# A mixer block with an FFT convolution: step two's matrix loaded twice from 64 rows, and a new order of loads and work in the first chunk

## The chip, the cores and the metric

The kernel runs on one core of a Trainium2 chip. Such a core has five engines with queues of their own: TensorE (matrix products; loading weights and streaming the moving operand are separate instructions), VectorE, ScalarE, GpSimd (called POOL in the profile) and SyncE, which here only issues transfers. SBUF is the working memory of 128 partitions, PSUM holds TensorE's results. The metric is device time in microseconds (us) of one execution, lower is better.

## The reference

Inputs are q, k, v of 2048 tokens × 640 channels, all float32. The reference, cut to what matters:

```python
def _A_ref(q, k, v, shift_k, ssm_k, ssm_D):
    k_shift = sum(k_pad[:, t:t + S, :] * shift_k[:, ks - 1 - t] for t in range(ks))   # ks = 4
    kv = k_shift * v
    kv_f = rfft2(kv_pad); kf_f = rfft2(kf_pad)           # length 2 S = 4096, per channel
    y = irfft2(kv_f * kf_f)[:S] + kv * ssm_D
    return q * y

x = A_q
sa, ca, ga, sb, cb, gb = split(_silu(c) @ w_mod, 6)      # "modulation", 640 each
h = _layernorm(x) * (1 + ca) + sa
x = x + ga * _A_ref(h, A_k, A_v, A_shift_k, A_ssm_k, A_ssm_D)
h = _layernorm(x) * (1 + cb) + sb
x = x + gb * _B_ref(h, B_w1, B_b1, B_w2, B_b2)           # MLP over tokens, hidden size 1728
```

## The kernel before

**Tiling.** The 640 channels are worked in five chunks of 128 (`NC`, `DC`), one after the other. Each chunk's K·V product and its filter go through a Fourier transform that is written as two matrix steps, are multiplied, and come back through two inverse steps. After the fifth chunk follow the second layer norm and the MLP, which the change does not touch.

**One chunk.** The stages, with the lines that the profile gives:

- `kv_ops(g)` (L59, four groups g): the short convolution times v, eight operations a group, into `X` (tile x). Groups 0, 1 and 3 run on VectorE with the taps copy `TAP` in PSUM, group 2 on POOL with the taps copy `PW` in SBUF. `taps()` and `all_taps()` make these copies, and `load_taps`, `load_k`, `load_v`, `load_halo` load what they read. `kv_loads(c, g)` issues the loads for the next chunk behind group g.
- `step1(side, t)` (L218): step one, side 0 from `X`, side 1 (the filter) from `KSP` (tile p); 32 matmuls for each of four t, whose moving operand is the constant `F1`. The weights of side 0 are a view of `X` whose 64 columns lie 32 floats apart; those of side 1 lie side by side. ScalarE copies each result to `T_z` (L220).
- `load_ks`, `perm_add`, `perm` bring the filter of a chunk: load, add `ssm_D` to one row, and reorder on ScalarE (L164).
- `f2(g)` (L234): step two, eight groups of 64 matmuls. The weights are 64 columns of the constant matrix `T_w2` (two tiles of 128 × 4096, the tiles w0 and w1 of the trace's w), the moving operand is a view of `T_z`. Each weight slice is loaded twice in a row, once for each half of the output partitions. Then ScalarE copies a part out (L238), VectorE multiplies (p), and POOL adds (y), VectorE in the last group of chunks one to four.
- `i2` (L263) and `i1` (L282): the inverse steps. `i1` uses the constant `V1`, whose place `T_v1` also holds pieces of `w_mod` in the first chunk.
- `gate` multiplies by the normalised x (`A1`, made by the operations `ac` on ScalarE and `po` on VectorE) and adds into x on POOL; `spill` writes x away.

**The first chunk** also computes the layer norm's statistics (L536, L537), `rstd`, and the first half of the modulation: `mod_load` (w_mod, five parts), `mod_part` (products, L342), `mod_sum`, `mod_row` (L353 to L369). In it, `step1(0, t)` for the second chunk runs right behind the first chunk's step two, and `step1(1, t)` for the second chunk at its end.

**Order.** The schedule is written by hand: every engine's queue holds its instructions in the order of the program, and each waits for what it reads or overwrites. `fill` is a list of VectorE operations (the next chunk's `kv_ops`), and `dv(n)` puts the next n of them into the program. SyncE's queue holds nearly all transfers, so a transfer that waits holds up those behind it; a few early ones are issued from ScalarE's queue. PSUM results rotate through three slots (`psum()`), and `tap` is a fourth of its own that holds the taps and also the modulation's sum.

**The matrix.** The constant `c_w2` has 128 rows of 8192 floats. A row stands for a part (real or imaginary), an index n2 and a channel parity; half of its entries are zero, because a channel's outputs take nothing from the other parity.

Of the kernel before, what the change touches and what calls it, by code (L numbers as in the profile page):

```python
# [11 lines left out]
AF = mybir.ActivationFunctionType  # L12
# [8 lines left out]
def _constants():  # L21


    n1, n2, k1, k2 = np.arange(64), np.arange(32), np.arange(64), np.arange(32)
    a = 2 * np.pi * ((1 + 4 * k1)[None, :] * n1[:, None] % 256) / 256
    f1 = np.zeros((2, 64, 2, 2, 64))
    for h in range(2):
        f1[h, :, 0, h], f1[h, :, 1, h] = np.cos(a), np.sin(a)
    ang = 2 * np.pi * ((1 + 4 * k1)[None, :, None] * n2[:, None, None] / 8192
                       + (k2[None, None, :] * n2[:, None, None] % 32) / 32)  # L30
    w2 = np.zeros((2, 32, 2, 64, 2, 2, 32))
    for c in range(2):
        w2[0, :, c, :, 0, c] = np.cos(ang)
        w2[1, :, c, :, 0, c] = -np.sin(ang)
        w2[0, :, c, :, 1, c] = np.sin(ang)
        w2[1, :, c, :, 1, c] = np.cos(ang)
    ang = 2 * np.pi * (k2[:, None] * n2[None, :] % 32) / 32
    c, s = np.cos(ang), np.sin(ang)
    v2 = np.tile(np.concatenate([c, -s, s, c], 1), (4, 1))
    ang = 2 * np.pi * ((1 + 4 * k1)[:, None, None] * (32 * n1[None, None, :] + n2[None, :, None]) % 8192) / 8192  # L40
    v1 = np.tile(np.stack([np.cos(ang), np.sin(ang)], 1).reshape(64, 4096) / 2048, (2, 1))
    sel = np.zeros((128, 128))
    sel[0, 0:64] = sel[1, 64:128] = 1
    small = np.concatenate([f1.reshape(128, 256), v2, np.eye(128)[:, 0:36], sel], 1)
    return {"small": small.astype(np.float32), "w2": w2.reshape(128, 8192).astype(np.float32),
            "v1": v1.astype(np.float32)}


# [1 line left out]
def mixer_kernel(ctx: ExitStack, tc: tile.TileContext, q, k, v, shift_k, ssm_k, ssm_D, w1, b1, w2, b2, c,  # L50
# [24 lines left out]
    def dram(t, offset, ap):  # L75
        return bass.AP(tensor=t.tensor, offset=t.offset + offset, ap=ap)
# [18 lines left out]
    Z = T_z.rearrange("p (s t a k e) -> p s t a k e", s=2, t=4, a=8, e=2)  # L95
    T2 = T_z[:, 4096:8192].rearrange("p (a m e) -> p a m e", a=32, e=2)
    Y = T_y.rearrange("p (r i k) -> p r i k", r=2, i=32)
    W2 = [t.rearrange("p (k m) -> p k m", m=64) for t in T_w2]
    V1 = T_v1[:, 0:4096].rearrange("p (r n m) -> p r n m", r=2, n=32)
    SM = T_v1[:, 4096:4516]  # L100
    F1, V2, ID = SM[:, 0:256], SM[:, 256:384], SM[:, 384:420]
# [44 lines left out]
    def load_taps(c, eng=sync):  # L146
        for h in range(2):
            eng.dma_start(TR[64 * h:64 * h + 64], dram(shift_k, (DC * c + 64 * h) * 4, [[0, 64], [1, 256]]))
# [75 lines left out]
    def f2(g):  # L224

        ps = psum()
        for kk in range(8):
            k1 = 8 * g + kk
            for ri in range(2):
                for h in range(2):  # L230
                    o = 128 * kk + 64 * ri
                    rhs = bass.AP(tensor=T_z.tensor, offset=T_z.offset + 128 * h + 2 * k1,
                                  ap=[T_z.ap[0], [256, 32], [1, 2]])
                    pe.matmul(ps[64 * h:64 * h + 64, o:o + 64], W2[k1 // 32][:, 2 * (k1 % 32) + ri], rhs, start=True, stop=True)  # L234
        pv = ps.rearrange("p (m s i) -> p m s i", s=2, i=32)
        xs_ = pv[:, :, 0]
        kt = KT[g % 2]
        act.activation(kt.rearrange("p (m i) -> p m i", i=32), pv[:, :, 1], AF.Copy)  # L238
        pa, pb = P[:, 1024 * (g % 2):1024 * (g % 2) + 512], P[:, 1024 * (g % 2) + 512:1024 * (g % 2) + 1024]
        m16 = lambda t: t.rearrange("p (m i) -> p m i", i=32)  # L240

        def mul():
            TT(dve, m16(pa), xs_, m16(kt), ALU.mult)
            sw = bass.AP(tensor=kt.tensor, offset=kt.offset + 32, ap=[kt.ap[0], [64, 8], [-32, 2], [1, 32]])
            TT(dve, pb.rearrange("p (k r i) -> p k r i", k=8, r=2), xs_.rearrange("p (k r) i -> p k r i", r=2), sw,
               ALU.mult)
# [187 lines left out]


    piece = lambda t, n: [t[:, 640 * i:640 * i + 640] for i in range(n)]
    stg = T_g[0:36, 0:128]
    dve.memset(stg, 0.0)
    dve.memset(ones, 1.0)
    dve.memset(msk, 1.0)  # L440
    dve.memset(msk[0:32], 0.0)
    dve.memset(epsc, EPS)
    for h in range(2):
        dve.memset(KX[64 * h:64 * h + 1, 0:3, :], 0.0)
    both = (sync, act)
# [13 lines left out]
    def run(ops):  # L459
        for f_ in ops:  # L460
            f_()
# [2 lines left out]
    all_taps()  # L464
    load_taps(1, act)
    run(kv_ops(2, pool))
    run(kv_ops(0))
    kv_loads(1, 0)
    run(kv_ops(1))
    kv_loads(1, 1)  # L470
    kv_loads(1, 2)
    run(kv_ops(3))
    sync.dma_start(T_w2[0], c_w2[:, 0:4096], max_dma_last_dim=4096)
    kv_loads(1, 3)
    sync.dma_start(T_w2[1], c_w2[:, 4096:8192], max_dma_last_dim=4096)
    for h in range(2):
        sync.dma_start(stg[7 * h:7 * h + 6, :], dram(b1, 864 * h, [[128, 6], [1, 128]]))
        sync.dma_start(stg[7 * h + 6:7 * h + 7, :], dram(b1, 864 * h + 736, [[128, 1], [1, 128]]))
    sync.dma_start(stg[14:30, :], dram(b2, 0, [[128, 16], [1, 128]]))
    sync.dma_start(stg[30:35, :], dram(c, 0, [[128, 5], [1, 128]]))  # L480
    perm_add(0)
    perm(0)
    all_taps()
    load_taps(2)
    for t in range(4):
        step1(0, t)
    run(kv_ops(2, pool))
# [2 lines left out]
    for t in range(4):  # L490
        step1(1, t)

    for j in range(0, 16, 2):
        for b in range(2):
            sync.dma_start(XH[j // 8][64 * b:64 * b + 64, j % 8:j % 8 + 2],
                           dram(q, (16 * b + j) * D, [[32 * D, 64], [D, 2], [1, D]]))
# [14 lines left out]
    for c in range(NC):  # L511
# [30 lines left out]
        if c == 0:  # L542
            mod_load(0, 4, P[:, 0:1920])
            for t in range(4):
                step1(0, t)
            ps = psum()
            pe.transpose(ps[:, 0:36], stg, ID[0:36, 0:36])
            act.activation(cols, ps[:, 0:36], AF.Copy)
            act.activation(sil, cols[:, 30:35], AF.Silu)
            i2(0)  # L550
            for kk in range(4):
                mod_part(tap, kk, pl[kk])
                if kk == 0:
                    load_ks(1)
            sync.dma_start(T_v1[:, 0:4096], c_v1, max_dma_last_dim=4096)
            rstd(rs1, nm1, 0, 16)
            run(ac[0:4])
            i2(1)
            mod_part(tap, 4, pl[4])
            load_k(2, 1)  # L560
            load_k(2, 2)
            load_v(2, 2)
            load_halo(2)
            load_k(2, 0)
            load_v(2, 0)
            load_v(2, 1)
            load_k(2, 3)
            load_v(2, 3)
            mod_sum(tap, T_kt[:, 0:640])
            run(ac[4:8])  # L570
            pool.tensor_scalar(PW, TR.rearrange("p (i s) -> p s i", s=4), 1.0, None, op0=ALU.mult)
            run(kv_ops(2, pool))
            for i in range(3):
                mod_row(i, T_kt[:, 0:640])
            taps()
            load_taps(3)
            perm_add(1, dve)
            perm(1)
            load_ks(2)
            run(ac[8:16])  # L580
            run(po[0:2])
            fill.extend(kv(3, ((0,), (1, 2), (3,))))
        elif cn is not None:
            for t in range(2):
                step1(0, t)
            perm(cn)
            if c + 2 < NC:
                fill.extend(kv(c + 3 if c + 3 < NC else None))
            else:
                fill.extend(x1s(cc, j) for cc in range(c) for j in range(16))  # L590
        else:
            blk.update({f: (j16(t[:, 0:2048]), j16(t[:, 2048:4096])) for f, t in (
                (0, mem("w0", 4096, "wb0")), (1, mem("w1", 4096, "wb1")))})
            mod_load(3, 3, T_z[:, 0:1920])
            mod_load(3, 4, P[:, 0:1920])
            for kk in range(3):
                mod_part(tap, kk, pl[kk])
            t = mem("in", 4288, "wb3")
            blk[3] = j16(t[:, 0:2048]), j16(t[:, 2048:4096])
            split_rows(0, X, (0, 1, 3))  # L600
            split_rows(1, T_aux[:, 0:2048], (0, 1, 3))
            run(po)
# [36 lines left out]
        spill(c)  # L639
        if c:  # L640
            k0()
        for t in range(1 if c else 0, 4):
            step1(1, t)
        if cn == NC - 1:
# [24 lines left out]
    start = []  # L669
# [410 lines left out]
```

## Time and profile before

| what | us |
|---|---|
| median of 3 runs (lowest, highest) | 722.62 (722.25, 728.29) |
| the profiled execution's own time | 726.87 |
| its span, first to last instruction | 725.0 |
| step two of the second chunk begins | 115.58 |
| step two of the third, fourth, fifth chunk begins | 166.47, 216.14, 273.93 |
| mean granted TensorE clock | 0.968 |

In a group line of the profile stand the source line, the engine, the operation, the tile written and the tiles read, the shapes and the count; then the busy time with the mean length of one in ns; then the idle time of the engine just ahead, and what ended it. `PE` is TensorE's matmul, `PEld` its weight load, `SPq` and `ACTq` are issues in SyncE's and ScalarE's queue. A timeline row has start and length in us, and merges neighbours of one kind (x32: 32 of them); in square brackets stands the idle time before it. Since matmuls overlap in time, the length of one says little about their rate.

### The profile page before, as it was taken

Reading aid. Unit: us, or ns where it says so; the run is one execution under the profiler, and the core shown is the slowest. Engines: PE = TensorE matmul, PEld = TensorE weight load, DVE = VectorE, ACT = ScalarE, POOL = GpSimd, SP = SyncE. Lnnn points to the kernel's source line nnn. Section 1 sums busy time; section 2 is a strip of 40 time slices with the busy share of each in tenths; the row PEclk is TensorE's granted clock in tenths of the full one; section 3 lists DMA queues with packets and bytes.
Section 4 is the critical chain, followed back from the end, with each engine's and each line's share of the span. In section 5 each row is a group of like instructions: output and inputs, shape, how many; then the busy total and the mean of one; then the engine's idle time right before and its main releaser. Section 6 shows DMA issues by size and latency. Waiting matters only on the chain.

```text
span 725.0 us, 20744 instructions
## 1 busy us (share of the span) xinstructions
PE 655.3 (90%) x9131; PEld 633.1 (87%) x9131; DVE 493.4 (68%) x861; ACT 297.1 (41%) x461; POOL 155.0 (21%) x135
## 2 busy tenths in 40 slices
PE   0797969999999989888799999999999989999997
PEld 0797759989989979767799999999999989999997
DVE  7766658969878537878895312311399868878887
ACT  0532565645645535544766313212335222332222
POOL 5197048625428226300000000000000000000000
PEclk9999889999999889989999999999999999999999
DMA  9989998345423440352112453353163433455410
GB/s 187 242 232 233 298 230 178 91 75 140 87 65 114 113 107 15 111 114 63 29 31 59 80 95 60 59 105 70 51 189 103 129 100 117 140 157 175 149 54 37
DMA packets 165807, 84.89 MB, mean 117 GB/s; under 512 B 88883, under 2 KB 157270, under 8 KB 165718
## 3 DMA queue, kind: packets, MB, share of 16 engines
q1 hardware_dynamic: 161170, 82.27, 45.8%
q10 hardware_dynamic: 4548, 1.31, 1.1%
q8 instruction: 71, 1.16, 0.7%
q14 instruction: 18, 0.15, 0.1%
HBM read 73.07 MB, written 10.49 MB: 115 GB/s over the span
## 4 chain that ended last, share of the span: by engine, by line
PE 53%; DVE 24%; issue 6%; ACT 6%; POOL 4%; DMA 4%; SPq 2%; ACTq 0%; DVEq 0%; POOLq 0%
PE pst L432 21%; PE pst L218 9%; PE pst L1021 7%; PE pst L234 6%; PE pst L263 5%; DVE m_w L59 4%; POOL y L59 4%; PE pst L282 3%; DVE m_x L59 3%; DVE tap L59 2%; ACT m_w L934 2%; PE pst L946 2%; DVE kt L59 2%; DVE m_v L59 1%; DVE m_x L955 1%
## 5 line engine op out<-in xcount | busy, mean ns | idle before, releaser
L234 PE MATMUL pst<-z,w 128*64 128x64 f32 x2560 | 96.2, 240 | 10.6 <-ACT z L220 6.1
L234 PEld LDWEIGHTS pst<-z,w 128*64 128x64 f32 x2560 | 94.8, 141 | 12.4 <-ACT z L220 7.3
L59 POOL TENSOR_TENSOR y<-p 128x256 f32<-128x256 f32 x72 | 91.2, 1319 | 28.3 <-DVE p L59 27.9
L59 DVE TENSOR_TENSOR p<-pst,kt 128x512 f32<-128x512 f32 x80 | 52.7, 691 | 29.6 <-ACT kt L238 20.3
L218 PE MATMUL pst<-v,x 128*64 128x128 f32 x640 | 48.0, 312 | 23.6 <-DVE x L59 23.2
L220 ACT ACTIVATE z<-pst 128x1024 f32<-128x1024 f32 x40 | 45.8, 1145 | 55.3 <-PE pst L218 33.7
L218 PEld LDWEIGHTS pst<-v,x 128*64 128x64 f32 x640 | 45.7, 221 | 24.3 <-POOL t L457 23.2
L238 ACT ACTIVATE kt<-pst 128x512 f32<-128x512 f32 x40 | 25.2, 629 | 57.6 <-PE pst L234 37.7
L825 ACT ACTIVATE pst<-pst,sm 128x640 f32<-128x640 f32 x14 | 10.7, 767 | 85.9 <-PE pst L432 85.9
L263 PEld LDWEIGHTS pst<-v,y 32*128 32x128 f32 x1280 | 40.8, 198 | 5.9 <-POOL y L59 2.7
L263 PE MATMUL pst<-v,y 32*128 32x64 f32 x1280 | 42.9, 284 | 2.7 <-DVE y L59 1.9
L946 PE MATMUL pst<-r_z,m_w 128*128 128x320 f32 x222 | 42.8, 312 | 2.2 <-DVE m_w L59 1.7
L218 PE MATMUL pst<-v,p 128*64 128x128 f32 x640 | 40.0, 284 | 2.2 <-issue 2.2
L218 PEld LDWEIGHTS pst<-v,p 128*64 128x64 f32 x640 | 37.5, 143 | 3.4 <-issue 2.9
L934 ACT ACTIVATE m_w<-m_v 128x896 fp32r<-128x896 f32 x24 | 22.2, 949 | 42.3 <-DVE m_v L59 29.4
L946 PEld LDWEIGHTS pst<-r_z,m_w 128*128 128x128 f32 x222 | 34.9, 189 | 3.8 <-DVE m_w L59 3.0
L59 DVE TENSOR_TENSOR tap<-tap,kt 128x512 f32<-128x512 f32 x51 | 35.6, 698 | 1.3
L59 DVE TENSOR_TENSOR kt<-in,tap 128x512 f32<-128x512 f32 x51 | 35.0, 686 | 1.4
L282 PEld LDWEIGHTS pst<-z,v 64*64 64x64 f32 x1280 | 23.6, 152 | 11.7 <-issue 6.2
L282 PE MATMUL pst<-z,v 64*64 64x64 f32 x1280 | 25.3, 238 | 9.3 <-issue 4.9
L59 DVE TENSOR_TENSOR m_w<-m_v,m_w 128x896 fp32r<-128x896 f32 x24 | 26.0, 1087 | 10.4 <-ACT m_w L934 10.4
L271 ACT ACTIVATE z<-pst 128x512 f32<-128x512 f32 x38 | 21.2, 657 | 26.4 <-PE pst L263 26.4
(276 smaller groups left out, 1422.5 us busy)
## 6 DMA issues: line engine op xcount, KB each, us to landing
x<-in_B_w_dram SPq DMA_DIRECT2D x24, 512.0 KB
m_v<-in_B_w_dram SPq DMA_DIRECT2D x15, 384.0 KB
x<-in_B_w_dram SPq DMA_DIRECT2D x14, 384.0 KB
aux<-in_A_ssm_k_dram SPq DMA_DIRECT2D x10, 512.0 KB
in<-in_A_k_dram SPq DMA_DIRECT2D x36, 128.0 KB
in<-in_A_v_dram SPq DMA_DIRECT2D x36, 128.0 KB
m_x<-xs SPq DMA_DIRECT2D x28, 160.0 KB
out_dram<-m_x SPq DMA_DIRECT2D x28, 160.0 KB
```

What stands on the lines that cost most here:

```text
L59: TT = lambda eng, o, a, b, op: eng.tensor_tensor(o, a, b, op=op)
L218: pe.matmul(ps[64 * ri:64 * ri + 64, o:o + 128], lhs, F1[:, 128 * ri:128 * ri + 128], start=True, stop=True)
L220: evac = lambda: act.activation(Z[:, side, t].rearrange("p a k e -> p e a k"), ps.rearrange("p (e a k) -> p e a k", a=8, e=2), AF.Copy)
L234: pe.matmul(ps[64 * h:64 * h + 64, o:o + 64], W2[k1 // 32][:, 2 * (k1 % 32) + ri], rhs, start=True, stop=True)
L238: act.activation(kt.rearrange("p (m i) -> p m i", i=32), pv[:, :, 1], AF.Copy)
L263: pe.matmul(pp[qd // 2][:, o:o + 64], Y[p, ri, i:i + 2].rearrange("p i k -> p (i k)"), V2[p, 64 * ri:64 * ri + 64], start=ri == 0, stop=ri ...
L271: act.activation(o, i, AF.Copy)
L282: pe.matmul(ps[64 * b:64 * b + 64, 512 * e + 64 * jj:512 * e + 64 * jj + 64], V1[p, ri, n2], T2[p, :, 32 * ri + n2], start=ri == 0, stop=r ...
L432: pe.matmul(ps[0:m, h, 0:320], w_.bitcast(F32R), r_[:, 320 * h:320 * h + 320].bitcast(F32R), start=first and i == 0, stop=last and i == 2)
L934: act.activation(W[n][0].bitcast(F32R), a(w_), AF.Copy)
L946: pe.matmul(bank[n], w[:, i].bitcast(F32R), r.bitcast(F32R), start=i == 0 and k == 0, stop=i == 6 and k == 2)
L1021: pe.matmul(acc[s][:, h, 0:320], w[:, f_].bitcast(F32R), u[r + h].bitcast(F32R), start=f_ == 0 and k == 0, stop=f_ == NF - 1 and k == 2)
```

## The change

Six things are done. The zeros of the matrix are no longer loaded: the constant has 64 rows of 4096, each half of it is written twice, into the even and the odd partitions of a tile that POOL has set to zero. So that both copies are runs of memory, the tile's columns now lie with the matrix's column as the outer index: a weight slice's 64 columns lie 64 floats apart (`w2_of`). The order of transfers in the first chunk is new: the first half of the matrix ahead of the second chunk's K and V, the second half behind all of them, the biases, c and a set of taps moved from there into the loop over q, and q loaded one row index at a time (32 transfers in place of 16). 72 matmuls whose result nobody reads stand ahead of the first step one, and a small ScalarE copy stands at the start. Inside the first chunk, the third chunk's K and V, its POOL group and 16 VectorE operations are moved ahead, the second filter's load behind that of `V1`, and its `perm_add`, `perm` and the next filter's load behind the gate work. The modulation's sum uses a rotating PSUM slot instead of `tap`.

```diff
-    w2 = np.zeros((2, 32, 2, 64, 2, 2, 32))
...
+    w2 = np.zeros((2, 32, 64, 2, 32))
+    w2[0, :, :, 0], w2[1, :, :, 0] = np.cos(ang), -np.sin(ang)
+    w2[0, :, :, 1], w2[1, :, :, 1] = np.sin(ang), np.cos(ang)
...
-    W2 = [t.rearrange("p (k m) -> p k m", m=64) for t in T_w2]
+    def w2_of(k1, ri):
+        return T_w2[k1 // 32].rearrange("p (m k) -> p k m", m=64)[:, 2 * (k1 % 32) + ri]
+
+    def load_w2c(i):
+        for e in range(2):
+            sync.dma_start(T_w2[i][e::2, 2048 * e:2048 * e + 2048], c_w2[:, 2048 * i:2048 * i + 2048],
+                           max_dma_last_dim=4096)
...
-                    pe.matmul(ps[64 * h:64 * h + 64, o:o + 64], W2[k1 // 32][:, 2 * (k1 % 32) + ri], rhs, start=True, stop=True)
+                    pe.matmul(ps[64 * h:64 * h + 64, o:o + 64], w2_of(k1, ri), rhs, start=True, stop=True)
...
+    pool.memset(T_w2[0], 0.0)
     stg = T_g[0:36, 0:128]
...
     dve.memset(epsc, EPS)
+    act.activation(tm[:, 0:1], epsc, AF.Copy)
...
     run(kv_ops(2, pool))
+    pool.memset(T_w2[1], 0.0)
+    load_w2c(0)
     run(kv_ops(0))
...
     run(kv_ops(3))
-    sync.dma_start(T_w2[0], c_w2[:, 0:4096], max_dma_last_dim=4096)
     kv_loads(1, 3)
-    sync.dma_start(T_w2[1], c_w2[:, 4096:8192], max_dma_last_dim=4096)
-    (b1, b2 and c into stg: six transfers)
+    load_w2c(1)
     perm_add(0)
     perm(0)
     all_taps()
-    load_taps(2)
+    ps = psum()
+    for i in range(72):
+        pe.matmul(ps[0:64, 0:128], F1[:, 0:64], F1[:, 128:256], start=True, stop=True)
...
-    for j in range(0, 16, 2):
+    for j in range(16):
         for b in range(2):
-            sync.dma_start(XH[j // 8][64 * b:64 * b + 64, j % 8:j % 8 + 2],
-                           dram(q, (16 * b + j) * D, [[32 * D, 64], [D, 2], [1, D]]))
+            sync.dma_start(XH[j // 8][64 * b:64 * b + 64, j % 8], dram(q, (16 * b + j) * D, [[32 * D, 64], [1, D]]))
+        if j == 11:
+            (b1, b2 and c into stg: six transfers)
+            load_taps(2)
...
+            taps()
+            pool.tensor_scalar(PW, TR.rearrange("p (i s) -> p s i", s=4), 1.0, None, op0=ALU.mult)
             i2(0)
-            for kk in range(4):
-                mod_part(tap, kk, pl[kk])
-                if kk == 0:
-                    load_ks(1)
-            sync.dma_start(T_v1[:, 0:4096], c_v1, max_dma_last_dim=4096)
-            rstd(rs1, nm1, 0, 16)
-            run(ac[0:4])
-            i2(1)
-            mod_part(tap, 4, pl[4])
             load_k(2, 1)
...
             load_v(2, 3)
-            mod_sum(tap, T_kt[:, 0:640])
+            load_taps(3)
+            mt = psum()
+            for kk in range(4):
+                mod_part(mt, kk, pl[kk])
+            sync.dma_start(T_v1[:, 0:4096], c_v1, max_dma_last_dim=4096)
+            load_ks(1)
+            rstd(rs1, nm1, 0, 16)
+            run(kv_ops(2, pool))
+            run(ac[0:4])
+            i2(1)
+            mod_part(mt, 4, pl[4])
+            mod_sum(mt, T_kt[:, 0:640])
+            fill.extend(kv(3, ((0,), (1, 2), (3,))))
+            dv(16)
             run(ac[4:8])
-            pool.tensor_scalar(PW, TR.rearrange("p (i s) -> p s i", s=4), 1.0, None, op0=ALU.mult)
-            run(kv_ops(2, pool))
             for i in range(3):
                 mod_row(i, T_kt[:, 0:640])
-            taps()
-            load_taps(3)
-            perm_add(1, dve)
-            perm(1)
-            load_ks(2)
             run(ac[8:16])
             run(po[0:2])
-            fill.extend(kv(3, ((0,), (1, 2), (3,))))
...
         if c:
             k0()
+        else:
+            perm_add(1, dve)
+            perm(1)
+            load_ks(2)
```

More of the change, by code (lines that the diff above doesn't have):

```diff
@@ L30, in _constants @@
                        + (k2[None, None, :] * n2[:, None, None] % 32) / 32)
-    w2 = np.zeros((2, 32, 2, 64, 2, 2, 32))
[L32 to L36, printed above, removed]
+    w2 = np.zeros((2, 32, 64, 2, 32))
+    w2[0, :, :, 0], w2[1, :, :, 0] = np.cos(ang), -np.sin(ang)
+    w2[0, :, :, 1], w2[1, :, :, 1] = np.sin(ang), np.cos(ang)
     ang = 2 * np.pi * (k2[:, None] * n2[None, :] % 32) / 32
@@ L44, in _constants @@
     small = np.concatenate([f1.reshape(128, 256), v2, np.eye(128)[:, 0:36], sel], 1)
-    return {"small": small.astype(np.float32), "w2": w2.reshape(128, 8192).astype(np.float32),
+    return {"small": small.astype(np.float32), "w2": w2.reshape(64, 2, 64, 32).transpose(0, 1, 3, 2).reshape(64, 4096).astype(np.float32),
             "v1": v1.astype(np.float32)}
@@ L472, in mixer_kernel @@
     run(kv_ops(3))
-    sync.dma_start(T_w2[0], c_w2[:, 0:4096], max_dma_last_dim=4096)
     kv_loads(1, 3)
-    sync.dma_start(T_w2[1], c_w2[:, 4096:8192], max_dma_last_dim=4096)
[L476 to L480, printed above, removed]
+    load_w2c(1)
     perm_add(0)
@@ L491, in mixer_kernel @@
         step1(1, t)
-    for j in range(0, 16, 2):
+    for j in range(16):
         for b in range(2):
-            sync.dma_start(XH[j // 8][64 * b:64 * b + 64, j % 8:j % 8 + 2],
-                           dram(q, (16 * b + j) * D, [[32 * D, 64], [D, 2], [1, D]]))
+            sync.dma_start(XH[j // 8][64 * b:64 * b + 64, j % 8], dram(q, (16 * b + j) * D, [[32 * D, 64], [1, D]]))
+        if j == 11:
+            for h in range(2):
+                sync.dma_start(stg[7 * h:7 * h + 6, :], dram(b1, 864 * h, [[128, 6], [1, 128]]))
+                sync.dma_start(stg[7 * h + 6:7 * h + 7, :], dram(b1, 864 * h + 736, [[128, 1], [1, 128]]))
+            sync.dma_start(stg[14:30, :], dram(b2, 0, [[128, 16], [1, 128]]))
+            sync.dma_start(stg[30:35, :], dram(c, 0, [[128, 5], [1, 128]]))
+            load_taps(2)
     three = lambda t: [t[:, 640 * j:640 * j + 640] for j in range(3)]
```

## The prediction

> **What bounds the kernel now.** I read the page's engine shares, its chain and its groups first, then the timeline around each stage that the diff touches, then single lines.
>
> ```profile
> PE 655.3 (90%) x9131; PEld 633.1 (87%) x9131; DVE 493.4 (68%) x861; ACT 297.1 (41%) x461; POOL 155.0 (21%) x135
> PE 53%; DVE 24%; issue 6%; ACT 6%; POOL 4%; DMA 4%; SPq 2%; ACTq 0%; DVEq 0%; POOLq 0%
> L234 PEld LDWEIGHTS pst<-z,w 128*64 128x64 f32 x2560 | 94.8, 141 | 12.4 <-ACT z L220 7.3
> L59 POOL TENSOR_TENSOR y<-p 128x256 f32<-128x256 f32 x72 | 91.2, 1319 | 28.3 <-DVE p L59 27.9
> L218 PEld LDWEIGHTS pst<-v,x 128*64 128x64 f32 x640 | 45.7, 221 | 24.3 <-POOL t L457 23.2
> L59 DVE TENSOR_TENSOR tap<-tap,kt 128x512 f32<-128x512 f32 x51 | 35.6, 698 | 1.3
> ```
>
> TensorE carries half of the chain. Step two (L234, 2,560 matmuls, 512 in each of five chunks) loads weights for 94.8 us. Its stationary operand is the matrix that the diff lays anew, so all five chunks matter, not the first alone. Matmul durations overlap, so I take speed from the distance of starts: how often step one's copy out of PSUM (ACT z, one for 32 matmuls) comes.
>
> ```profile
> 29.12 1.16 ACT L220 ACTIVATE z<-pst 128x1024 f32<-128x1024 f32 x1 [0.97 <-PE pst L218]
> 31.17 1.15 ACT L220 ACTIVATE z<-pst 128x1024 f32<-128x1024 f32 x1 [0.90 <-PE pst L218]
> 33.18 1.14 ACT L220 ACTIVATE z<-pst 128x1024 f32<-128x1024 f32 x1 [0.86 <-PE pst L218]
> 34.93 1.14 ACT L220 ACTIVATE z<-pst 128x1024 f32<-128x1024 f32 x1 [0.60 <-PE pst L218]
> 36.67 1.14 ACT L220 ACTIVATE z<-pst 128x1024 f32<-128x1024 f32 x1 [0.61 <-PE pst L218]
> ...
> 166.47 19.02 PE L234 MATMUL pst<-z,w 128*64 128x64 f32 x511 [1.24 <-ACT z L220]
> ```
>
> ```profile
> L218 PEld LDWEIGHTS pst<-v,x x79: 199/221/238, 27.8 to 32.7; 128*64 128x64 f32 x79
> L218 PEld LDWEIGHTS pst<-v,p x123: 137/137/137, 33.1 to 39.8; 128*64 128x64 f32 x123
> ```
>
> Here step one runs twice on the same moving matrix. With weights taken out of `X` (64 columns, 32 floats apart) copies lie 2.05 and 2.01 us apart, 63.4 ns a matmul; with weights out of `P` (64 columns side by side) 1.74 us, 54.4 ns. Minimum, median and maximum of a load are 199/221/238 ns against 137 throughout. Step two's columns now lie side by side too: 19.02 us / 511 = 37.2 ns a matmul.
>
> The first chunk's rows, in order:
>
> ```profile
> 0.71 1.19 ACTq L148 DMA_DIRECT2D rows<-in_A_shift_k_dram  x2
> 0.94 0.11 DVE L439 MEMSET sm<- 128x64 f32 x1
> 20.96 1.28 ACT L164 ACT_TABLE_LOAD   x1 [20.96 <-DMA in<-in_A_k_dram]
> 23.22 9.92 PE L218 MATMUL pst<-v,x 128*64 128x128 f32 x128 [23.22 <-DVE x L59]
> 26.96 1.19 ACT L220 ACTIVATE z<-pst 128x1024 f32<-128x1024 f32 x1 [2.60 <-PE pst L218]
> ...
> 37.16 2.52 POOL L59 TENSOR_TENSOR t<-in,t 128x512 f32<-128x512 f32 x2 [14.61 <-DMA in<-in_A_k_dram]
> 41.30 13.11 PE L234 MATMUL pst<-z,w 128*64 128x64 f32 x349 [1.17 <-ACT z L220]
> ...
> 46.06 5.08 SPq L495 DMA_DIRECT2D xa<-in_A_q_dram  x8
> 48.10 17.05 POOL L59 TENSOR_TENSOR y<-p 128x256 f32<-128x256 f32 x14
> 67.17 0.88 DVE L536 BATCH_NORM_STATS2 sm<-xa 128x6 f32<-128x320 f32 x2
> ...
> 83.04 0.21 DVE L537 BATCH_NORM_AGGREGATE sm<-sm 128x2 f32<-128x12 f32 x1
> 85.21 0.25 DVE L317 RECIPROCAL sm<-sm 128x16 f32<-128x16 f32 x1 [1.96 <-ACT sm L326]
> 96.51 1.56 DVE L59 TENSOR_TENSOR g<-pst,g 128x640 f32<-128x640 f32 x2 [9.78 <-ACT g L360]
> 97.98 0.53 DVE L59 TENSOR_TENSOR aux<-aux,rows 1x64 f32<-1x64 f32 x2
> 98.54 2.48 DVE L59 TENSOR_TENSOR aux<-aux,g 128x1024 f32<-128x1024 f32 x2
> 98.60 2.15 ACT L164 ACTIVATE p<-aux 128x2048 f32<-128x2048 f32 x1 [1.00 <-issue]
> ...
> 102.33 1.23 DVE L59 TENSOR_TENSOR aux<-pst,aux 128x1024 f32<-128x1024 f32 x1 [1.30 <-PE pst L282]
> 103.83 4.50 DVE L59 TENSOR_TENSOR aux<-aux,g 128x1024 f32<-128x1024 f32 x2 [0.27 <-ACT aux L289]
> ...
> 113.52 2.37 POOL L59 TENSOR_TENSOR xa<-xa,aux 128x1024 f32<-128x1024 f32 x1
> 114.44 1.09 ACT L220 ACTIVATE z<-pst 128x1024 f32<-128x1024 f32 x1 [0.59 <-PE pst L218]
> 115.58 9.62 PE L234 MATMUL pst<-z,w 128*64 128x64 f32 x256 [1.18 <-ACT z L220]
> ```
>
> and three pieces of the chain (start, length):
>
> ```profile
> 59.65 3.93 issue
> 63.58 1.60 PE pst L234 x36
> ...
> 84.48 2.79 SPq L152
> 87.31 2.31 SPq L155
> ...
> 90.51 7.94 DMA v<-in_const_v_dram
> ```
>
> Step two of the first chunk runs from 41.30 to 65.18 with a stall of 3.93 us in it; that of the second starts at 115.58. Between them the end is set by TensorE, by SyncE issuing the next K filter's loads, then by the load of `V1`. VectorE waits 9.78 us there.
>
> **The change part by part.**
>
> *The new layout, chunks two to five.* The 64 columns of a load of L234 now lie 64 floats apart. No row shows that distance; the nearest is `X`'s 32. I take step two's pace to be that of loads spread out. Step one's 63.4 ns is above what its moving side needs (54.4 at the most), so there the load is the limit, and a shorter moving side cannot make it faster: 63.4 ns. That adds 26.2 ns × 512 = 13.4 us a chunk. The low bound is nothing, should such loads hide; between them lies the bare difference of the two step-one paces, 9.0 ns, 4.6 us a chunk. The high bound adds the whole 84 ns by which a load lengthens (221 − 137), shared by the two column halves: 42 ns, 21.5 us. Not hidden: TensorE is back to back here, 511 matmuls in 19.02 us. One thing is given back. POOL's two additions a group (2 × 1.319 us) lag now behind 64 × 37.2 ns = 2.38 us; behind 4.06 us they won't, and I estimate 0.5 us saved at the end of three chunks, 1.5 us. Sum: 4 × 13.4 − 1.5 = +52.2 us.
>
> The Trainium skill's page "TensorE: Matmul & The Clock Gate", section "LDWEIGHTS (loading the stationary operand)", has a load's time go by its number of columns alone. By that rule the layout is free, and it is the first rival below. The two rows of loads, 221 and 137 ns for 64 columns each, do not agree with it as it stands.
>
> *Start.* ScalarE's new small copy stands ahead of its DMA issues (first at 0.71). It waits for the memset of `epsc` behind the one at 0.94, and it brings the table load, 1.28 us, forward from 20.96, where it had cover. Taps and half of K then go out 0.5 to 2.1 us later, and the first matmul waits for VectorE's K·V work on them until 23.22, so this passes on: I take 1.2. The 72 idle matmuls on `F1` may take away the slow first group (3.74 us from 23.22 to 26.96, then 2.05): 0 to 1.6, I take 0.8; if `F1` lands late they delay step one instead. The two POOL memsets of 4,096 elements a row: from 3.4 us each (VectorE's 0.11 us for 64, less its fixed part, 0.84 ns each) to 9.5 (POOL's two-input 2.37 us for 1,024). The nearest in kind, one output without an input, is the lower. The first has until the taps land and costs nothing at that; at the upper end `kv_ops` on POOL starts some 2.5 us late. The second stands ahead of `perm_add(0)` and so of `perm(0)` on ScalarE, in front of the first copy at 26.96: nothing at 3.4, and at 9.5 some 2 us at the start of step two. So step two begins at 41.30 + 1.2 − 0.8 = 41.7.
>
> *Loads.* 4 MiB of matrix become 2 MiB. `V1`, 2 MiB, took 7.94 us, so this is about 8 us of the queue. On SyncE the first half of the matrix passes ahead of the second chunk's K and V; the third K and V pass ahead of the other half, which is what POOL waits 14.61 us for at 37.16. The 16 extra q issues cost SyncE 16 × 5.08 / 8 = 10.2 us, which the removed 8 us mostly pay; the small vectors and taps only change their place behind q. I cost these at nothing, because the pieces of the chain shown hold no load between 41 and 84; without that cover they would cost those 10.2 us. The stall of 3.93 us I let go, since the same instructions are spread over more time.
>
> *First step two.* 512 × 63.4 ns = 32.5 us, from 41.7 to 74.2 instead of 65.18.
>
> *Between first and second.* The filter's loads leave the way of `V1`, which goes out right behind the first four parts of the modulation, at about 92, and lands at 100. The third chunk's K and V pass ahead of it on SyncE, and are through by then. But VectorE gets 16 of the third chunk's K·V operations ahead of the modulation rows, and `perm_add(1)`, which stood in front of the gate work at 97.98, is now behind it; step one's second half and everything after it wait for that. From the end of step two: 2.0 to the first statistics (65.18 to 67.17), 16.1 for them (67.17 to 83.25), 3.5 to the end of the reciprocal root (86.73, where the 9.78 us wait begins), 16 operations of 0.698 us with gaps 11.5, the rows 1.56, the scaling 2.48, the gate 1.23, scaling again 4.5, gate 1.23, `perm_add` 0.53, `perm` 2.15, step one 128 × 54.4 ns with a slow first group (+1.6) 8.6, copy 1.1: 56.5 us. So 74.2 + 56.5 = 130.7 against 115.58: +15.1. `V1`'s way, 100 plus the first step of the inverse, ends before VectorE is ready. The 16 operations taken out of the second chunk's step two lay under TensorE there and give nothing back.
>
> *Sum.* 52.2 + 15.1 = +67.3 us. The profiled execution spans 725.0 us and took 726.87; its new span would be 792. The median of the runs shown is 722.62, so 790.
>
> **The rivals.**
>
> *The layout is free.* Step two stays at 19.0 us; in the first chunk POOL starts its additions some 4 us before 48.10 (1 MiB less ahead of its K), needs 12 of them (15.8) before the last group's products (1.4), and so holds the end at about 62; 62 + 56.5 = 118.5, +2.9, less 0.5 in the second chunk: 725. For it: nobody has shown 64 floats. Against it: 221 and 137 ns.
>
> *The load is only partly in the way* (+9.0 ns): 512 × 46.2 = 23.7 us, second step two at 41.7 + 23.7 + 56.5 = 121.9, +6.3; chunks after it 18.4 − 1.5. Together +23.2: 746. For it: the same 9.0 ns is all that step one shows.
>
> *The load is wholly in the way* (79.2 ns): 40.6 us, second step two at 138.8, +23.2; after it 86 − 1.5: 830. For it: the 84 ns. Against it: step one hid most of them.
>
> *Faster.* The layout is free and VectorE's 16 operations fit into its 9.78 us wait, so that `V1`'s way alone decides: it loses the issue time ahead of it (84.48 to 90.51, 6.0) and the first step two's stalls (23.9 − 19.2 = 4.7). That is −10.7: 712. It decides only if a group of step two stays below POOL's 2.64 us, that is at under 41 ns a matmul. Against it: both `X` rows.
>
> **How the numbers follow.** Forecast 0.60, partly 0.13, wholly 0.11, free 0.12, faster 0.04. About 1% is what a measurement of this kernel can tell from no change. Slower by over that hold the first three: 0.84; within it the free layout: 0.12; faster: 0.04. The range takes in the three slower cases, with POOL's and ScalarE's bounds: 742 to 835.
>
> **What would show it.** Loads of L234 at about 220 ns instead of 141, and 64 of its matmuls in about 4 us instead of 2.4, in every chunk; POOL's additions with gaps; VectorE without its 9.78 us wait and `perm_add(1)` behind the gates; step two of the second chunk at about 130. If L234 keeps its 19 us, all of this falls but the first chunk's few microseconds. If the loads lengthen and the pace doesn't, the load was hidden.

## The result, and the profile after

The changed kernel takes 823.88 us (median of 4 runs, 822.07 to 824.21). The kernel before, run beside it, takes 725.45 us (722.25 to 728.88). The ratio is 1.133, 95% interval 1.1283 to 1.1377. The profiled execution spans 821.1 us, 96.1 more than before.

The page of the changed kernel: engine totals, the chain's shares, and three groups (L239 is now step two, L489 are the 72 idle matmuls).

```profile
PE 756.1 (92%) x9275; PEld 735.0 (90%) x9275; DVE 494.6 (60%) x861; ACT 296.2 (36%) x462; POOL 162.6 (20%) x137
PE 67%; DVE 18%; ACT 5%; issue 4%; SPq 2%; DMA 2%; POOL 1%; DVEq 0%; ACTq 0%
L239 PEld LDWEIGHTS pst<-z,w 128*64 128x64 f32 x2560 | 187.1, 251 | 7.3 <-ACT z L225 7.3
L57 POOL TENSOR_TENSOR y<-p 128x256 f32<-128x256 f32 x72 | 93.5, 1323 | 119.3 <-DVE p L57 119.3
L489 PE MATMUL pst<-v 128*64 128x128 f32 x144 | 18.1, 294 | 14.4 <-DMA v<-in_const_small_dram 14.4
```

Weight loads of step two last 251 ns instead of 141 and are busy for twice as long, with the same count. POOL's idle time ahead of its additions grew from 28 to 119 us: it now waits for VectorE's products of step two. And 72 matmuls in the program are 144 in the trace: a float32 product leaves two records. All counts of matmuls and loads in this text, and all times "a matmul", go by records: a group of step two is 32 products of the program and 64 records, a part of step one 16 and 32.

TensorE's timeline of the same kernel (start, length) shows every step two, the idle matmuls, and the long wait in the first chunk.

```profile
14.42 18.00 PE L489 MATMUL pst<-v 128*64 128x128 f32 x143 [14.42 <-DMA v<-in_const_small_dram]
...
48.74 37.52 PE L239 MATMUL pst<-z,w 128*64 128x64 f32 x512 [1.17 <-ACT z L225]
...
118.07 5.41 PE L287 MATMUL pst<-z,v 64*64 64x64 f32 x253 [2.96 <-DMA v<-in_const_v_dram]
...
136.35 9.85 PE L223 MATMUL pst<-v,p 128*64 128x128 f32 x128 [10.69 <-ACT p L169]
147.43 37.57 PE L239 MATMUL pst<-z,w 128*64 128x64 f32 x512 [1.23 <-ACT z L225]
...
214.13 37.58 PE L239 MATMUL pst<-z,w 128*64 128x64 f32 x512 [1.25 <-ACT z L225]
...
280.68 37.53 PE L239 MATMUL pst<-z,w 128*64 128x64 f32 x512 [1.24 <-ACT z L225]
...
352.62 37.58 PE L239 MATMUL pst<-z,w 128*64 128x64 f32 x512 [1.23 <-ACT z L225]
```

Step two takes 37.5 us a chunk, 73.3 ns a matmul, where it took 19.0. From these starts and those of before, the 96.1 us divide like this (each number is the growth of one distance):

| distance | before | after | growth |
|---|---|---|---|
| start to the first step two | 41.30 | 48.74 | 7.4 |
| first to second step two | 74.28 | 98.69 | 24.4 |
| second to third | 50.89 | 66.70 | 15.8 |
| third to fourth | 49.67 | 66.55 | 16.9 |
| fourth to fifth | 57.79 | 71.94 | 14.2 |
| fifth to the end | 451.07 | 468.48 | 17.4 |

So 64.3 us fall in the last four rows, where nothing but the layout differs inside step two; step two itself is 18.5 us longer there, and 1 to 4 us of each come back between the steps. The other 31.8 us are in the first chunk: 7.4 at the start, 13.6 in step two (37.52 us after 23.88, stalls included), and 10.8 between its end and the second step two.

Most of the 10.8 us lies in TensorE's wait of 10.69 us, which ends at 136.35. It waits for `perm`, which waits for `perm_add(1)`, and that now stands behind the gate work on VectorE. VectorE has no gap of more than 0.4 us from 87.06, behind step two's last copy, to there; its timeline in the changed kernel:

```profile
108.89 0.68 DVE L57 TENSOR_TENSOR tap<-in,tap 128x512 f32<-128x512 f32 x1
...
119.85 0.69 DVE L57 TENSOR_TENSOR x<-tap,in 128x512 f32<-128x512 f32 x1
120.45 1.55 DVE L57 TENSOR_TENSOR g<-pst,g 128x640 f32<-128x640 f32 x2
122.03 2.48 DVE L57 TENSOR_TENSOR aux<-aux,g 128x1024 f32<-128x1024 f32 x2
124.62 1.23 DVE L57 TENSOR_TENSOR aux<-pst,aux 128x1024 f32<-128x1024 f32 x1
125.77 4.49 DVE L57 TENSOR_TENSOR aux<-aux,g 128x1024 f32<-128x1024 f32 x2
130.36 1.23 DVE L57 TENSOR_TENSOR aux<-pst,aux 128x1024 f32<-128x1024 f32 x1
```

From 108.89 to 120.54 run the 16 operations, then the rows, the scalings and the gates, and `perm_add` from 131.50 (shown at the end). SyncE's queue waits as well:

```profile
90.15 0.37 SPq L340 DMA_DIRECT2D p<-in_w_mod_dram  x1
90.57 3.35 SPq L137 DMA_DIRECT2D in<-in_A_k_dram  x4
93.96 3.68 SPq L143 DMA_DIRECT2D in<-in_A_v_dram  x2
...
105.50 1.21 SPq L153 DMA_DIRECT2D rows<-in_A_shift_k_dram  x2
106.97 0.40 SPq L577 DMA_DIRECT2D v<-in_const_v_dram  x1
107.42 11.38 SPq L157 DMA_DIRECT2D aux<-in_A_ssm_k_dram  x2
```

The fifth part of `w_mod` may overwrite tile p only when POOL has done its last addition, at 90.13. All of the third chunk's K and V stand behind it, and `V1` behind those: it goes out at 106.97, and `i1`, which reads it, starts at 118.07. In this kernel that costs little. The queue is free at 106.71, and the modulation's products, which still read `V1`'s place, end only at 106.91:

```profile
104.59 2.32 PE L347 MATMUL pst<-v,sm 128*32 128x320 f32 x24
```

TensorE then waits 2.96 us for `V1`, and the gate at 124.62 shows no wait for `i1`. `V1` decides only where step two is short again, in the experiments below.

### The profile page after: what moved, and what is told of

It is laid out like the page before. It is cut to its first block, busy times and chain, and to the rows that moved or that the text cites. A ratio compares the mean times of both kernels' runs of the same rounds, so it can differ in the third digit from the quotient of the medians.

```text
span 821.1 us, 21080 instructions
## 1 busy us (share of the span) xinstructions
PE 756.1 (92%) x9275; PEld 735.0 (90%) x9275; DVE 494.6 (60%) x861; ACT 296.2 (36%) x462; POOL 162.6 (20%) x137
## 4 chain that ended last, share of the span: by engine, by line
PE 67%; DVE 18%; ACT 5%; issue 4%; SPq 2%; DMA 2%; POOL 1%; DVEq 0%; ACTq 0%
PE pst L239 23%; PE pst L437 18%; PE pst L223 9%; PE pst L1034 6%; DVE m_w L57 4%; PE pst L268 4%; PE pst L287 2%; DVE m_x L57 2%; PE pst L489 2%; ACT m_w L947 2%; PE pst L959 1%; DVE aux L57 1%; DVE m_v L57 1%; DVE m_x L968 1%; DVE m_p L57 1%
## 5 line engine op out<-in xcount | busy, mean ns | idle before, releaser
L239 PEld LDWEIGHTS pst<-z,w 128*64 128x64 f32 x2560 | 187.1, 251 | 7.3 <-ACT z L225 7.3
L239 PE MATMUL pst<-z,w 128*64 128x64 f32 x2560 | 187.8, 312 | 6.1 <-ACT z L225 6.1
L57 POOL TENSOR_TENSOR y<-p 128x256 f32<-128x256 f32 x72 | 93.5, 1323 | 119.3 <-DVE p L57 119.3
L223 PEld LDWEIGHTS pst<-v,p 128*64 128x64 f32 x640 | 37.6, 144 | 11.2 <-ACT p L169 10.8
L223 PE MATMUL pst<-v,x 128*64 128x128 f32 x640 | 43.2, 291 | 1.4 <-issue 1.4
L223 PEld LDWEIGHTS pst<-v,x 128*64 128x64 f32 x640 | 41.2, 218 | 2.0 <-issue 1.6
L268 PE MATMUL pst<-v,y 32*128 32x64 f32 x1280 | 41.1, 278 | 0.6 <-ACT z L225 0.6
L489 PE MATMUL pst<-v 128*64 128x128 f32 x144 | 18.1, 294 | 14.4 <-DMA v<-in_const_small_dram 14.4
```

Of the source, the lines that this page charges most:

```text
L57: TT = lambda eng, o, a, b, op: eng.tensor_tensor(o, a, b, op=op)
L223: pe.matmul(ps[64 * ri:64 * ri + 64, o:o + 128], lhs, F1[:, 128 * ri:128 * ri + 128], start=True, stop=True)
L239: pe.matmul(ps[64 * h:64 * h + 64, o:o + 64], w2_of(k1, ri), rhs, start=True, stop=True)
L268: pe.matmul(pp[qd // 2][:, o:o + 64], Y[p, ri, i:i + 2].rearrange("p i k -> p (i k)"), V2[p, 64 * ri:64 * ri + 64], start=ri == 0, stop=ri ...
L489: pe.matmul(ps[0:64, 0:128], F1[:, 0:64], F1[:, 128:256], start=True, stop=True)
```

## The experiments

Each kernel was timed beside the kernel before on the same chip; a time is a median unless it is called a single run.

**b_col64: the layout alone.** The kernel before, with the matrix stored the other way round.

```diff
-w2.reshape(128, 8192)
+w2.reshape(128, 2, 1, 64, 64).transpose(0, 1, 2, 4, 3).reshape(128, 8192)
-W2 = [t.rearrange("p (k m) -> p k m", m=64) for t in T_w2]
+W2 = [t.rearrange("p (a m b) -> p a b m", m=64, b=64) for t in T_w2]
```

> The kernel before with one edit: the matrix is stored so that the 64 columns of a weight slice lie 64 floats apart; its 128 rows, its two loads and the whole order of the first chunk stay. Theory (the layout makes each weight load of step two longer and sets its pace): step two takes about 37.5 us a chunk instead of 19.0, loads of about 251 ns; the distance from one chunk's step two to the next grows by 14 to 17 us as in the changed kernel; total 785 to 805 us. Rival (the pace comes from what is new around it: half tiles set to zero and written in every second partition, the new order, the queues): step two stays at 19.0 us and the total at 722 to 727.

Measured: 802.35 us beside 728.54, ratio 1.1013 (1.0956 to 1.107). TensorE's timeline of this kernel:

```profile
41.56 37.57 PE L234 MATMUL pst<-z,w 128*64 128x64 f32 x512 [1.17 <-ACT z L220]
...
125.06 37.52 PE L234 MATMUL pst<-z,w 128*64 128x64 f32 x512 [1.19 <-ACT z L220]
...
193.87 37.57 PE L234 MATMUL pst<-z,w 128*64 128x64 f32 x512 [1.24 <-ACT z L220]
```

The same 37.5 us, with old loads, old order and no memset. The rival that the surroundings make the pace falls. The layout alone carries 10.1 of the 13.3 per cent.

**b_col4 and b_col2: other distances.** The same edit with `b=4` and `b=2` in the view and the store.

> The kernel before with the columns of a weight slice 4 floats (16 bytes) apart. If any distance other than side by side costs the same, step two takes 37.5 us a chunk and the total is that of b_col64. If a load pays only from some distance on, it is between 19.0 and 37.5 us; if 16 bytes are still free, 19.0 and 722 to 727 in total.

> The kernel before with the columns of a weight slice 2 floats (8 bytes) apart. At 4 floats step two took 31.2 us a chunk, at 64 floats 37.5, side by side 19.0. If a load is free while two of its columns share 16 bytes (the Trainium skill's rule on lines), step two takes 19.0 to 20 us and the total is that of the kernel before. If any distance costs, it takes 25 to 31 us and the total is 745 to 770.

Measured: 770.05 us for 4 (a single run, beside 728.54), 724.45 for 2 (a single run, beside 725.66). The weight loads of step two by line, first of b_col4, then of b_col2, then of b_col64 (minimum/median/maximum in ns):

```profile
L234 PEld LDWEIGHTS pst<-z,w x2560: 193/217/227, 40.9 to 338.1; 128*64 128x64 f32 x197
```

```profile
L234 PEld LDWEIGHTS pst<-z,w x2560: 136/145/224, 41.9 to 292.0; 128*64 128x64 f32 x197
```

```profile
L234 PEld LDWEIGHTS pst<-z,w x2560: 217/252/254, 41.6 to 368.9; 128*64 128x64 f32 x197
```

And one step two of each in TensorE's timeline, b_col4 and then b_col2:

```profile
182.32 31.17 PE L234 MATMUL pst<-z,w 128*64 128x64 f32 x512 [1.25 <-ACT z L220]
```

```profile
167.77 19.57 PE L234 MATMUL pst<-z,w 128*64 128x64 f32 x512 [1.24 <-ACT z L220]
```

Two floats apart is almost free (38.2 ns a matmul against 37.2), four cost 60.9 ns, sixty-four 73.3. The step lies between 8 and 16 bytes, and there is more to pay further out. The Trainium skill's page "SBUF — State Buffer", section "Door 1: The DMA port swizzle", speaks of lines of 16 bytes that need at least two accesses each for full speed. The two runs agree with that. The same note lets float32 stride four elements for free; here four cost 12.2 us a chunk (31.17 − 19.0).

**b_xside: the same rule on step one.** The kernel before, with `X` stored so that step one's columns lie side by side; the K·V operations write it 256 bytes apart.

```diff
-X.rearrange("p (n i)", i=64)[:, 8 * g:8 * g + 8], S_, VX[...]
+X.rearrange("p (i n s) -> p n s i", i=32, s=2)[:, 8 * g:8 * g + 8], four(S_), four(VX[...])
-X.rearrange("p (m i) -> p i m", i=32)[:, i]
+X.rearrange("p (i m) -> p i m", i=32)[:, i]
```

> The kernel before with X stored so that step one's 64 weight columns lie side by side; VectorE and POOL write X with their elements 256 bytes apart instead. If the layout rule is general, step one from X goes from 63.4 to 54.4 ns a matmul, 1.2 us a chunk of 128 matmuls, and loads from 221 to 137 ns; total 717 to 722 if the writes cost no more than 0.1 us each, 722 to 730 if they cost more.

Measured: 733.97 us beside 725.66, ratio 1.0109 (1.0057 to 1.0162). Step one's loads (L219 here), then the group of VectorE's writes:

```profile
L219 PEld LDWEIGHTS pst<-v,x x640: 132/137/232, 24.3 to 261.2; 128*64 128x64 f32 x160
```

```profile
L59 DVE TENSOR_TENSOR x<-tap,in 128x512 f32<-128x512 f32 x17 | 19.5, 1148 | 7.9 <-PE pst L219 7.5
```

The loads fall from 221 to 137 ns as expected, and ScalarE's copies come 1.75 us apart instead of 2.03. But a write of `X` takes 1,148 ns instead of 690, and the kernel is 1.1% slower, above both ranges that I gave. The strided side was moved, not removed.

**a_side: the change without its layout.** The old matrix of 128 rows, loaded whole at the new places, no memsets.

> The changed kernel with the old matrix (128 rows, columns side by side) loaded whole at the new places, and without the two memsets; all else of the change stays. Theory (the layout costs 64 us in chunks two to five and 18.5 in the first; the 72 idle matmuls and the later perm_add cost the rest): step two takes 19.0 us, begins at about 48.7 in the first chunk and at 127 to 130 in the second; total 732 to 740. Rival (the layout is all of the loss): total at or below 725.

Measured: 744.73 us beside 728.54, ratio 1.0207 (1.0133 to 1.0281). Step two is back at 19.1 us, and begins at 47.83 and 132.71. Against the kernel beside it 16.2 us are left, where I had reckoned with some 7 to 15: the first chunk loses on its own. Behind the shorter step two TensorE now waits 9.46 us for `V1`, and 8.32 for `perm`.

**a_nodummy: the change without the 72 idle matmuls.**

```diff
-    ps = psum()
-    for i in range(72):
-        pe.matmul(ps[0:64, 0:128], F1[:, 0:64], F1[:, 128:256], start=True, stop=True)
```

> The changed kernel without the 72 idle matmuls. Theory (they hold step one back from about 24 to 32.2 us): step two of the first chunk begins at 40 to 42 instead of 48.7, all that follows moves by as much, total 813 to 817. Rival (the K and V work or a transfer holds step one back anyway, and the matmuls warm the clock): step one begins no earlier than 31, total 822 or more.

Measured: 818.11 us (a single run). Step one begins at 24.66 instead of 32.16 and step two at 43.27 instead of 48.74: 7.5 us earlier in, 5.5 at step two, because without them the first step one is slow again (10.45 us for its 128 records; with them 8.4). They do make the first step one 2 us shorter, at a price of several times that. The granted clock reads 1.00 in both stretches, so the records do not say what made it slow. The end moved by 5.8 us, a little less than the lower bound that I gave.

**a_side_nodummy and a_side_pro: the order.** The first is a_side without the idle matmuls. The second has, besides, the kernel before's order of work between the first and the second step two, so that of the new order only the loads and the start remain.

> The changed kernel with the old matrix at the new places and without the 72 idle matmuls: what is left of the change is the order. Theory (the order inside the first chunk, with 16 K and V operations and the later perm_add ahead of step one, loses by itself): step two begins at about 41 in the first chunk and 124 to 127 in the second, against 41.3 and 115.6 before; total 733 to 738. Rival (the order gains, and only the idle matmuls spoiled it): second chunk at 112 to 115, total 718 to 722.

> As a_side_nodummy, but with the kernel before's order of the work between the first and the second step two; so the old matrix, the early first half of it, the third K and V ahead of the second half, q by rows and the small copy at the start remain. Theory (the loss of the order sits in that work): second step two at 113 to 117, total 720 to 726. Rival (it sits in the loads and the start): second step two at 120 or more, total 728 or more.

Measured: 743.25 us, ratio 1.023 (1.0172 to 1.0287), and 727.37 us, ratio 1.0033 (0.9999 to 1.0066), both beside 725.66. Both lie above the ranges I gave, the first by 5 us, the second by 1.4. The new loads, q by rows and the start are neutral to within 0.7%, and the reordered block loses about 16 us. With the layout mended, taking the idle matmuls out gains nothing that can be measured (ratio 1.023 after 1.0207). The traces show why: the first step two comes 4.6 us earlier (43.21 after 47.83), the second only 0.9 (131.78 after 132.71), since `V1` goes out 0.6 us earlier (96.93 after 97.51) and TensorE waits 12.34 us for it.

**a_nd_dv and a_nd_v1: what in the block.** a_nd_dv is a_side_nodummy without `dv(16)`. a_nd_v1 also has `V1`'s and the filter's loads ahead of the third chunk's K and V.

```diff
-            dv(16)
...
+            sync.dma_start(T_v1[:, 0:4096], c_v1, max_dma_last_dim=4096)
+            load_ks(1)
             load_k(2, 1)
...
             load_taps(3)
-            sync.dma_start(T_v1[:, 0:4096], c_v1, max_dma_last_dim=4096)
-            load_ks(1)
```

> As a_side_nodummy, without the 16 K and V operations ahead of the modulation rows; they run where the kernel before has them. If VectorE's order decides (16 operations, 11.6 us, then rows, gate, perm_add), second step two comes at 118 to 122 instead of 131.8 and the total at 728 to 734. If SyncE's queue decides (16 transfers ahead of V1's load, which goes out at 96.9 and lands at about 105), the gate still waits for the inverse step at 109 and the second step two stays at 128 to 131, total 738 to 743.

> As a_nd_dv, with V1's load and the second filter's loads ahead of the 16 K and V transfers in SyncE's queue; perm_add and perm stay behind the gates. If those transfers hold V1 back, it goes out at 86 to 90 instead of 99.9 and lands at 94 to 99 instead of 108.4; the gates come 9 to 12 us earlier and the second step two at 120 to 125 instead of 134.5, total 729 to 735. What is then left against the kernel before (115.6) is perm_add and perm behind the gates. If V1 is held by something else (the modulation's products, the transfer engines), it still lands after 104 and the total stays at 738 to 744.

Measured: a_nd_dv 742.9 us beside 726.41, ratio 1.0223 (1.016 to 1.0287): no better than with the 16 operations. a_nd_v1 731.24 us beside 727.1, ratio 1.0074 (1.0034 to 1.0114). VectorE's and TensorE's timeline of a_nd_dv, then SyncE's and TensorE's of a_nd_v1:

```profile
96.38 1.56 DVE L60 TENSOR_TENSOR g<-pst,g 128x640 f32<-128x640 f32 x2 [11.77 <-ACT g L366]
97.97 3.43 DVE L60 TENSOR_TENSOR aux<-aux,g 128x1024 f32<-128x1024 f32 x2
111.99 1.23 DVE L60 TENSOR_TENSOR aux<-pst,aux 128x1024 f32<-128x1024 f32 x1 [10.59 <-PE pst L288]
```

```profile
108.58 3.58 PE L288 MATMUL pst<-z,v 64*64 64x64 f32 x142 [12.94 <-DMA v<-in_const_v_dram]
...
123.73 9.49 PE L224 MATMUL pst<-v,p 128*64 128x128 f32 x128 [9.11 <-ACT p L170]
```

```profile
89.06 0.37 SPq L563 DMA_DIRECT2D v<-in_const_v_dram  x1
```

```profile
99.07 6.36 PE L288 MATMUL pst<-z,v 64*64 64x64 f32 x256 [2.14 <-DMA v<-in_const_v_dram]
110.39 9.07 PE L224 MATMUL pst<-v,p 128*64 128x128 f32 x128 [4.97 <-ACT p L170]
```

Without the 16 operations VectorE waits 11.77 and 10.59 us instead; with them it worked in that time. With `V1` out at 89.06, where it was 99.90, the second step two begins at 120.72 instead of 134.46 (for the latter I had given 128 to 131). With the mended layout, the order in SyncE's queue is what costs most. Of these 13.7 us, 9.5 are the earlier `i1`. The other 4.1 are TensorE's shorter wait for `perm`: POOL's K now comes late, POOL is idle until 109.33, and beside an idle POOL VectorE's two last scalings take 2.48 us instead of 4.50 and `perm_add` 0.53 instead of 2.68. About 5 us are left in that kernel, as long as TensorE's remaining wait of 4.97 us for `perm`. So `perm_add` and `perm` behind the gates account for them by the trace; putting them back alone was not tried, there or in the changed kernel.

**b_pair and b_v1act: two tries for something better.** b_pair is the kernel before with the change's 64 rows loaded twice, the two slices of one k1 interleaved so that columns lie 2 floats apart. b_v1act issues `V1` from ScalarE's queue.

```diff
+T_w2[k1 // 32].rearrange("p (k m r) -> p k r m", m=64, r=2)[:, k1 % 32, ri]
...
+sync.dma_start(T_w2[i][e::2].rearrange("p (k e x) -> p k e x", e=2, x=64)[:, :, e],
+               c_w2[:, 2048 * i:2048 * i + 2048].rearrange("p (k x) -> p k x", x=64))
```

> The kernel before with the change's saving kept and its layout mended: 64 rows loaded twice into zeroed tiles, but the two slices of one k1 interleaved, so that a slice's columns lie 2 floats apart and a load writes runs of 256 bytes. Theory (halving the bytes is worth up to 8 us of the queue, and nothing of it lies on the path): step two 19.5 us a chunk, total 720 to 728. Rival (the bytes were on the path): second step two at 108 to 112, total 715 to 719. Other rival (runs of 256 bytes and the even and odd partitions cost the queue more than the bytes save): K and V of the second chunk late, total 730 or more.

> The kernel before with one edit: V1's load is issued from ScalarE's queue behind the first four normalised rows, past the filter's loads in SyncE's queue. If SyncE's queue holds V1 back (issue at 90.51), the load goes out at about 88.6 and lands 2 us earlier, total 720 to 723 beside a before of 725. If both loads share the transfer engines, V1 lands no earlier, total 724 to 727.

Measured: b_pair 724.53 us beside 726.41, ratio 0.9975 (0.9942 to 1.0009); b_v1act 725.2 us, ratio 0.999 (0.9954 to 1.0027). In b_v1act the load goes out at 89.03, as expected, and `i1` still starts at 99.15: the load needs 10 us where it took 7.94, which fits the rival of shared transfer engines. Neither is measurably better than the kernel before. In b_pair step two takes 19.6 us a chunk instead of 19.0 and the second chunk's begins at 116.66, no earlier than before (115.58), so the halved bytes show no gain on the path; the interval leaves room for about 4 us in the total at most.

## Why the prediction was right or wrong

The direction, the main cause and its place were right: the layout sets step two's pace in all five chunks. The size was 790 us against 823.88. The span grew by 96.1 us where 67.3 were forecast, and the 28.8 us between them lie in four places: 12.1 behind the second step two, 7.0 at the start, 5.0 in the first step two, 4.7 between the first and the second. One step failed outright: the idle matmuls were given no length of their own. The other terms were of the right kind and mis-sized.

- **Step two's pace.** I took `X`'s 63.4 ns, for columns 32 floats apart, as the pace at 64 apart. It is 73.3. The reasoning that a load which shows through a longer moving side must limit a shorter one held: at 4 apart a load takes 217 ns, about `X`'s 221, and the pace is 60.9. The assumption that the distance doesn't matter beyond `X`'s did not. Step two grew by 18.5 us a chunk instead of 13.4, so 74 instead of 53.7 in chunks two to five.
- **What is given back.** I took 1.5 us; it is 74.0 − 64.3 = 9.7, and that the two errors partly cancel is luck. POOL's lag is the part that I named. The third chunk shows it: in the kernel before, the inverse step waited 0.72 us for the last addition, now it follows step one without a wait. Another part is TensorE's clock behind the fourth step two: before, 0.83 was granted from 255 to 275, and the last 96 records of step one took 7.75 us; in the changed kernel 1.00 was granted from 330 to 352, and they took 5.46. Why the clocks differ, no run shows. The rest was not taken apart.
- **The start of the first step two.** I forecast 41.7, it was 48.74. The step that failed is the one on the idle matmuls: I gave them a gain of 0 to 1.6 us and a loss only if `F1` came late. `F1` came at 14.42, early; the matmuls themselves last 18.0 us. I had not worked out their length: 144 records, all into one half of the output partitions, at 106 ns and more. The run without them shows 5.5 us of it. The start of ScalarE's issues cost 0.9 (first K and V operation at 6.65 instead of 5.71), within the 0.5 to 2.1 given.
- **POOL's memsets.** Each takes 3.51 us, near the lower of the two bounds. Neither is on the path: behind the first, POOL still waits 0.85 us for its taps, and behind the second, `perm` is done at 26.81, ahead of the first copy at 34.60.
- **Between first and second step two.** 56.5 us forecast; 147.43 − 86.26 = 61.2 measured. VectorE's path was the one forecast, link by link: statistics, 16 operations (11.5 forecast, 11.65 measured), rows, scalings, gates, `perm_add`, `perm`, step one. The missing 4.7 us are mainly three links: `perm_add` took 2.67 us beside POOL instead of 0.53; step one with its copy took 11.1 instead of 9.7, at a granted clock of 0.74 (136 to 147); and the reciprocal root 4.6 instead of 3.5. That `V1` would not decide held too, but not at the times given: I had it out 17.8 us behind the end of step two and landed 8 us later; by `i1`'s start it was 20.7 and 11.1. Where the gate waited for `i1`, it began 3.4 to 4.0 us behind `i1`'s start (before, a_side, a_side_nodummy, a_nd_dv). From 118.07 that is about 122, against 124.62, so I estimate that only some 3 of the 11.5 us would have come back without the 16 operations. In a kernel with the mended layout they cost nothing (a_nd_dv), because the gate waits for `V1` and `i1` there.
- **The loads.** Costing them at nothing was borne out: the loads and the start alone give 1.0033 (0.9999 to 1.0066), the halved bytes alone 0.9975 (0.9942 to 1.0009).

Of the rivals, the free layout and the gain through `V1` fell with 251 ns a load, and the load only partly in the way fell with 73.3 ns a matmul against its 46.2. The full-length one, 79.2 ns a matmul and 830 us, came nearer to the total than the forecast, by luck. It was not right in its terms: the pace is 73.3, and some 7 us of the total come from the late start, which it did not have.

## What to carry to other kernels

Look at the distance between the columns of a stationary operand, not only at its size: up to two float32 apart it is free here, from four on a matmul with a short moving side takes 1.6 to 2 times as long. A layout that suits a transfer of 2 MiB once is paid for by 2,560 records of weight loads, so count both sides, and where the other side writes instead (`X`), price its writes as well. When a transfer is moved ahead in a queue, look at what then stands behind it: `V1`, behind K and V, kept TensorE waiting 9 to 13 us once step two was short. And when a small operation is moved behind larger ones on its engine, see who reads its result: TensorE waited 10.69 us for `perm_add`'s.

## What the runs showed of the hardware that was not expected

- **One column half.** The idle matmuls, all into output partitions 0 to 63, come at 106 ns a record (94 records in the 10 us from 22 to 32 of the changed kernel, granted clock 1.00), while step one, alternating between the halves with a moving operand of the same 128 columns, takes 54.4. That the half is the reason is not shown: the idle matmuls also load the same weights and write the same place each time.
- **VectorE beside POOL.** The two one-row additions of `perm_add(1)` take 0.53 us together before, when POOL is idle. Beside POOL's addition into x they end when it does, 0.1 us behind it. Timeline of the changed kernel:

```profile
131.50 2.67 DVE L57 TENSOR_TENSOR aux<-aux,rows 1x64 f32<-1x64 f32 x2
131.72 2.34 POOL L57 TENSOR_TENSOR xb<-xb,aux 128x1024 f32<-128x1024 f32 x1 [2.55 <-DVE aux L57]
134.26 2.04 ACT L169 ACTIVATE p<-aux 128x2048 f32<-128x2048 f32 x1 [14.82 <-DVE aux L57]
```

The second addition alone lasts 2.40 us, until POOL is through, and ScalarE's `perm` waits for it. In a_nd_v1, where POOL is idle then, the two take 0.53 us again. The Trainium skill's page "SBUF — State Buffer", section "Who interferes with whom", has a VectorE instruction with two SBUF inputs contend with a GpSimd one that reads SBUF. These rows agree.
- **Strided writes.** VectorE's write of 512 floats 256 bytes apart takes 1,148 ns against 690 (b_xside).
